# Separate softmax sums for the plain heads, and the last score tile through the fused maximum, in an attention and mixture-of-experts kernel

## The chip, the cores and the metric

The kernel runs on one core of a Trainium2 chip, as one program. The metric is the device time of one execution in microseconds, the median over runs. Names of engines in the profile: PE is TensorE (PEld its weight loads), DVE is VectorE, ACT is ScalarE, POOL is GpSimd, SP is SyncE, which issues most transfers.

## The reference

```python
scores = q @ k^T / sqrt(64)                 # 4 batches, 8 heads, 576 tokens, 64 per head
scores = where(block_i >= block_j, scores, -1e9)   # blocks of 64 tokens
attn = exp(scores - max); attn = attn / (sum + 1e-9); x = attn @ v
x = x as 2304 tokens of 512
h = max(x @ w1, x @ w2, x @ w3); x = h @ w_out     # 512 -> 768 -> 512
logits = x @ w_gate + log1p(exp(x @ w_noise)) * noise
the two highest of 8 experts per token, softmax over the two
out = sum over both of weight * (relu(x @ w1[e]) @ w2[e])   # 512 -> 1024 -> 512
```

All data are fp32. The weights w1, w2, w3 and w_out arrive as 64-bit words, which the kernel turns into fp32 itself.

## The kernel before, in words

The program is written with a framework that places the waits and fixes, when the kernel is built, the order of the instructions on each engine: a planner with its own instruction times takes what is ready, by its place in the program text. The order in the trace is therefore near the text's, but not the same. On the chip each engine runs its queue in that fixed order.

**Attention.** A head has 576 queries. The first 256 (two tiles of 128, the "first" tiles) are computed apart from the rest; tiles 2, 3 and 4 are the head's three score steps. `s1` scores tile 2 against 384 keys, `s3` tile 3 against 512, `s2` tile 4 against 576, in two halves of 288 in a pair of PSUM banks called "a2" (one buffer). `s1` and `s3` share two banks called "s". The block mask is added by a small matmul (line 213) for the plain heads, and by the mask tile in the fused maximum for the others. The mask tile has 512 columns, all zero but for the upper half of the last 64.

Heads 0 to 7 (NF = 8, the first batch) are **plain**: fp32 products, then in `exps` a maximum on VectorE (line 240), a scaling by 0.125 of that maximum (line 241) and an exponential with its sum on ScalarE, read from PSUM (line 242). Heads 8 to 31 are **fused**: products in two fp32r parts, and for `s1` and `s3` one VectorE instruction (line 235) that adds the mask, writes the negated scaled scores to SBUF and keeps their minimum; the exponential then reads SBUF. `s2` takes the maximum and scaling in all heads before.

The three steps of one head share one statistics tile `st` (three buffers), made in `s2`. After the last step, `s3`, `inverse` (lines 245 and 246) adds 1e-9 to three sums and takes three reciprocals, and `scale_by` scales the three tiles: on VectorE (line 253), or on ScalarE (line 251) for `s3` of heads 0 to 2.

**First tiles.** Batch 0 does them for two heads at a time before the loop: `first_scores` (lines 432 to 447) gives four parts to `soft`, four times; `first_rest` turns them, multiplies with the values and writes the input of the gated layer's unit 0. The calls 1 and 3 have the bank pair "a2". Beside heads 1 to 4 `first_scores` runs four times more for batch 1. Batches 2 and 3 use `f_scores` with the fused maximum on two parts.

**The loop over heads** follows ORDER: in iteration i the score steps of head i + 1 and the transposes (`t1`, `t2`) and value products of head i are issued, with gaps ("g") in which weight conversion (`weights`) and, once the first weights are there, the gated layer (`filler`, with units in the order CH, lines 662 to 664) go in. This layer's matmuls are TensorE's filler during attention. Conversion of one piece of weight is a transfer and lines 575 to 588 on VectorE, ScalarE and GpSimd. After the loop come the rest of the gated layer, the routing and the experts (lines 1041 to 1090).

Of the kernel before, what the change touches and what calls it, by code (L numbers as in the profile page):

```python
# [13 lines left out]
AF = mybir.ActivationFunctionType  # L14
OP = mybir.AluOpType
AX = mybir.AxisListType
# [20 lines left out]
NF = 8  # L37
# [4 lines left out]
NRM = (0, 3, 0, 0)  # L42
# [7 lines left out]
NP, NK, NQ = 2, 2, 2  # L50
# [5 lines left out]
def plain(ap):  # L56
    return ap.bitcast(F32)
# [3 lines left out]
def tile_attention_moe_moe(ctx, tc, qT, kT, v, w1, w2, w3, w_out, gates, noise, e1, e2, out):  # L61
    nc = tc.nc
# [28 lines left out]
    mask = consts.tile([128, 512], BF, name="mask")  # L91
# [51 lines left out]
    PA = [att.tile([128, 384], F32, name=f"Pa{j}") for j in range(NP)]  # L143
    PB = [att.tile([128, 1088], F32, name=f"Pb{j}") for j in range(NP)]
# [44 lines left out]
    def prep_head(i):  # L189
        if i < NF:  # L190
            QK[i] = RAW.pop(i)
            return
        q, k = RAW.pop(i)
        Qs = att.tile([128, 384], F32R, name="Qs", bufs=NQ)
        Kh = att.tile([128, S], F32R, name="Kh", bufs=NK)
        Kl = att.tile([128, S], F32R, name="Kl", bufs=NK)
        nc.scalar.activation(Qs, q, AF.Copy)
        nc.scalar.activation(Kh, k, AF.Copy)
        nc.gpsimd.tensor_sub(Qs[64:], q[64:], plain(Qs[64:]))
        nc.gpsimd.tensor_sub(Kl, k, plain(Kh))  # L200
        QK[i] = (Qs, Kh, Kl)
# [9 lines left out]
    def masked(ps, o):  # L211

        nc.tensor.matmul(ps[:, o:o + 64], mL, mask[:, 448:], start=False, stop=True)

    def scores(ps, i, t, k0, k1, diag=None):
        if i < NF:
            q, k = QK[i]
            nc.tensor.matmul(ps, q[:D, 128 * t - 256:128 * t - 128], k[:D, k0:k1], start=True, stop=diag is None)
            if diag is not None:
                masked(ps, diag)  # L220
            return
        Qs, Kh, Kl = QK[i]
        lt = Qs[:, 128 * t - 256:128 * t - 128]
        nc.tensor.matmul(ps, lt, Kh[:, k0:k1], start=True, stop=False)
        nc.tensor.matmul(ps, lt, Kl[:, k0:k1], start=False, stop=True)

    def stats():
        return att.tile([128, 4, 4], F32, name="st", bufs=3)

    def exps(st, j, src, dst, fused):  # L230
        scale = 0.125
        if fused:

            w = src.shape[-1]
            nc.vector.tensor_tensor_reduce(out=dst, in0=src, in1=mask[:, 512 - w:], scale=-scale, scalar=3.0e38,
                                           op0=OP.add, op1=OP.min, accum_out=st[:, 1, j:j + 1])
            src, scale = dst, -1.0
        else:
            ax = AX.XY if len(src.shape) == 3 else AX.X
            nc.vector.tensor_reduce(st[:, 0, j:j + 1], src, axis=ax, op=OP.max, negate=True)  # L240
            nc.vector.tensor_scalar(st[:, 1, j:j + 1], st[:, 0, j:j + 1], scale, None, op0=OP.mult)  # L241
        nc.scalar.activation(dst, src, AF.Exp, bias=st[:, 1, j:j + 1], scale=scale, accum_out=st[:, 2, j:j + 1])

    def inverse(st, n):
        nc.vector.tensor_scalar(st[:, 2, :n], st[:, 2, :n], 1.0e-9, None, op0=OP.add)
        nc.vector.reciprocal(st[:, 3, :n], st[:, 2, :n])
        return st[:, 3]

    def scale_by(st, j, dst, norm=False):
        if norm:  # L250
            nc.scalar.activation(dst, dst, AF.Copy, scale=st[:, 3, j:j + 1])
        else:
            nc.vector.tensor_scalar(dst, dst, st[:, 3, j:j + 1], None, op0=OP.mult)

    def soft(parts, scaled=True, fused=False):
        st = stats()
        for j, (src, dst) in enumerate(parts):
            exps(st, j, src, dst, fused)
        inv = inverse(st, len(parts))
        if not scaled:  # L260

            return inv
        for j, (src, dst) in enumerate(parts):
            scale_by(st, j, dst)

    def bank(kind="m"):
        n, c = TAGS[kind]
        return (psS if n == "s" else psT).tile([128, 512], F32, name=n, bufs=c)


    ST = {}

    def s1(i):
        ps = bank("s")[:, :384]
        scores(ps, i, 2, 0, 384, 320)
        exps(ST[i], 1, ps, PA[i % NP], i >= NF)

    def s3(i):
        Pa, Pb, st = PA[i % NP], PB[i % NP], ST.pop(i)
        ps = bank("s")  # L280
        scores(ps, i, 3, 0, 512, 448)
        exps(st, 2, ps, Pb[:, 576:], i >= NF)

        inverse(st, 3)
        scale_by(st, 0, Pb[:, :576])
        scale_by(st, 1, Pa)
        scale_by(st, 2, Pb[:, 576:], i < NRM[1])

    def s2(i):
        Pb = PB[i % NP]  # L290
        ST[i] = stats()
        ps = psS.tile([128, 2, 512], F32, name="a2")
        scores(ps[:, 0, 0:288], i, 4, 0, 288)
        scores(ps[:, 1, 0:288], i, 4, 288, 576)
        exps(ST[i], 0, ps[:, :, 0:288], Pb[:, :576].rearrange("p (a b) -> p a b", a=2), False)

    POFF = {2: (PA, 0), 3: (PB, 576), 4: (PB, 0)}

# [133 lines left out]
    def first_scores(data, P, two=False, scaled=True):  # L432
        q, k = data[:2]
        parts = []
        if two:
            pair = psS.tile([128, 2, 512], F32, name="a2")
        for r in range(2):
            m = slice(64 * r, 64 * r + 64)
            ps = pair[:, r] if two else bank("s")
            for t in range(2):  # L440
                o = 128 * t
                n = o + 128
                a, b = (q, k[:, r]) if len(k.shape) == 3 else (q[m], k[m])
                nc.tensor.matmul(ps[:, o:o + n], a[:, o:o + 128], b[:, :n], start=True, stop=False)
                masked(ps, o + n - 64)
                parts.append((ps[:, o:o + n], P[:, 384 * r + o:384 * r + o + n]))
        return soft(parts, scaled)


    FR, FQ, FT = {}, {}, []  # L450
# [33 lines left out]
    def f_scores(b, h):  # L484
        Qs, Kh, Kl, _ = FQ[b, h]
        ps = bank("s")
        for t in range(2):
            p, lt = ps[:, 256 * t:256 * t + 256], Qs[:, 128 * t:128 * t + 128]
            nc.tensor.matmul(p, lt, Kh, start=True, stop=False)
            nc.tensor.matmul(p, lt, Kl, start=False, stop=True)  # L490
        soft([(ps[:, 0:128], FP[:, 0:128]), (ps[:, 256:512], FP[:, 128:384])], fused=True)
# [374 lines left out]
    def weights(n):  # L866
        for _ in range(n):
            next(conversion, None)

    weights(1)  # L870
    warm(bank(), WM[0])
    inv = first_scores(FIRST[0], PB[0], A2 & 1, False)
    for j in range(4):
        weights(WS[0])
        if j < 3:
            nxt = first_scores(FIRST[j + 1], PB[(j + 1) % NP], A2 >> (j + 1) & 1, False)
        first_rest(FIRST[j], PB[j % NP], PB[j % NP], 0, j, inv)
        inv = nxt
        weights(WS[1])
# [3 lines left out]
    load_head(1)  # L883
    load_values(1)
    weights(WS[4])
    s2(0)
    s1(0)
    s3(0)
    prep_head(1)
    weights(WS[2])  # L890
    cost = [0.0]
# [21 lines left out]
    for i in range(NH):  # L913
        b, h = divmod(i, H)
# [16 lines left out]
        for o in ORDER.split():  # L931
# [11 lines left out]
            elif o == "pf":  # L943
                if i + 1 in FI:
                    prep_f(*FI[i + 1])
                if i + 2 in FI:
                    load_f(*FI[i + 2])
            elif o == "fs":
                if i in AI:
                    first_scores(later.pop(), FP)  # L950
                    if order:
                        later.append(load_later(*order.pop(0)))
                if i in FI:
                    f_scores(*FI[i])
            elif o == "fr":
                if i - 1 in AI:
                    fb, j = AI[i - 1]
                    first_rest(now.pop(), FP, FP, 2 * fb, j)
                    if j == 3:
                        ready.add(2 * fb)  # L960
                if i in AI:
                    now.append([load_later_v(*AI[i])])
                if i - 1 in FI:
                    f_turn(*FI[i - 1])
            elif o == "fv":
                if i - 1 in FI:
                    f_values(*FI[i - 1])
            elif o[0] == "t":
                (t1, t2)[int(o[1]) - 1](i)
            elif i + 1 < NH:  # L970
                {"s1": s1, "s2": s2, "s3": s3}[o](i + 1)
# [16 lines left out]
    def bank2():  # L988
        turn[0] ^= 1
        if turn[0]:  # L990
            return ps2.tile([128, 512], F32, name="b")
        return psT.tile([128, 512], F32, name="t", bufs=4)
# [150 lines left out]
    ps = bank2()  # L1143
# [77 lines left out]
    with tc.If(full > 0):  # L1221
# [10 lines left out]
        with tc.For_i(0, E) as e:  # L1232
# [4 lines left out]
            with tc.For_i(0, NT) as t:  # L1237
# [6 lines left out]
                ps = ps3.tile([128, 4, 128], F32, name="pa")  # L1244
# [66 lines left out]
```

## Time and profile before

| | |
|---|---|
| median of 3 runs | 1087.37 us (1085.68 to 1087.65) |
| the profiled execution | 1087.95 us, span 1086.1 us |
| mean granted TensorE clock | 0.967 |
| TensorE busy | 1034.8 us (95%) |
| VectorE busy | 537.9 us (50%) |
| ScalarE busy | 459.1 us (42%) |
| GpSimd busy | 533.3 us (49%) |

The span is from the first to the last instruction; the time contains the little around it. Busy shares are means over stages of quite different kind: attention with conversion up to some 216 us, attention with the fused heads up to some 516 us, then the experts.

### The profile page before, as it was taken

What the parts mean: (1) busy time and instruction counts of PE and PEld (TensorE: products, weight loads), DVE (VectorE), ACT (ScalarE), POOL (GpSimd) and SP (SyncE); (2) the same over time, 40 slices, a digit from 0 to 9 for tenths busy, and PEclk for the clock granted to TensorE, in tenths of its full rate; (3) what the DMA queues carried; (4) which work ended last, traced back from release to release, by engine and by line L of the source; (5) the groups of instructions that cost most, each with busy time, mean ns of one, the idle gap of its engine ahead of it and who ended that gap; (6) DMA issues with size and microseconds to landing.
All of it is one profiled execution on the core that took longest, in us unless ns stands there. A gap on an engine that the chain in (4) does not pass through costs nothing. (4 is left out here: it accounts for less than half of the span.)

```text
span 1086.1 us, 18720 instructions
## 1 busy us (share of the span) xinstructions
PE 1034.8 (95%) x6721; PEld 917.4 (84%) x6721; DVE 537.9 (50%) x1552; ACT 459.1 (42%) x1138; POOL 533.3 (49%) x465
## 2 busy tenths in 40 slices
PE   8799999999979999799999999989999999999997
PEld 4466678998879989799999997979898898989895
DVE  7789746596796887756333632222132222222221
ACT  5656555565765666554311433323232322323110
POOL 4447503455556464451321448877474646656302
PEclk7698999998989999899999999999999999999999
DMA  9533312152442323211020236655443444443101
GB/s 232 160 93 125 106 47 63 34 157 58 144 150 65 113 63 100 70 26 39 24 80 21 69 118 206 198 167 169 130 159 121 143 146 146 137 136 114 57 20 63
DMA packets 78513, 115.93 MB, mean 107 GB/s; under 512 B 17976, under 2 KB 48184, under 8 KB 78416
## 3 DMA queue, kind: packets, MB, share of 16 engines
q1 hardware_dynamic: 67824, 85.28, 26.3%
q0 software_dynamic: 10592, 29.41, 8.3%
q8 instruction: 54, 0.88, 0.3%
q14 instruction: 43, 0.35, 0.1%
HBM read 95.18 MB, written 20.53 MB: 107 GB/s over the span
## 5 line engine op out<-in xcount | busy, mean ns | idle before, releaser
L132 POOL TENSOR_TENSOR w<-rw,w 128x1536 fp32r<-128x1536 f32 (+1 forms) x45 | 141.1, 3142 | 74.2 <-ACT w L131 63.9
L131 ACT ACTIVATE w<-rw 128x1536 fp32r<-128x1536 f32 (+1 forms) x45 | 60.2, 1343 | 114.4 <-DMA rw<-in_e 65.0
L662 PE MATMUL t<-xA,w 128*128 128x256 f32 x360 | 105.2, 294 | 1.5 <-ACT w L587 0.8
L664 PE MATMUL t<-xA,w 128*128 128x256 f32 x360 | 103.9, 289 | 0.0
L663 PE MATMUL t<-xA,w 128*128 128x256 f32 x360 | 103.7, 289 | 0.1
L1041 PE MATMUL b<-xh,w 128*128 128x384 f32 (+7 forms) x272 | 86.8, 320 | 0.9 <-ACT xh L1031 0.9
L1042 PE MATMUL b<-xl,w 128*128 128x384 f32 (+7 forms) x272 | 86.9, 320 | 0.2 <-DVE xl L1032 0.2
L1043 PE MATMUL b<-xh,w 128*128 128x384 f32 (+7 forms) x272 | 86.9, 319 | 0.0
L662 PE MATMUL t<-xB,w 128*128 128x256 f32 x288 | 83.7, 291 | 1.4 <-DVE st L241 1.2
L677 POOL TENSOR_TENSOR hl<-hm,hh 128x512 fp32r<-128x512 f32 x24 | 31.6, 1318 | 105.2 <-ACT hh L676 105.2
L663 PE MATMUL t<-xB,w 128*128 128x256 f32 x288 | 82.7, 287 | 0.0
L664 PE MATMUL t<-xB,w 128*128 128x256 f32 x288 | 82.3, 286 | 0.0
L1090 POOL DMA_INDIRECT out_rows<-y,isc x40 | 40.5, 1013 | 79.9 <-DVE y L1089 72.6
L1046 DVE SCALAR_TENSOR_TENSOR ht<-b,ht 128x384 fp32r<-128x384 f32 (+6 forms) x56 | 29.1, 519 | 97.5 <-ACT ht L1045 97.5
L669 DVE TENSOR_TENSOR hm<-t,hm 128x512 f32<-128x512 f32 x54 | 37.2, 690 | 72.1 <-PE t L664 64.1
L662 PEld LDWEIGHTS t<-xA,w 128*128 128x128 f32 x360 | 69.6, 194 | 3.7 <-ACT w L587 0.9
L1085 PE MATMUL b<-w,ht 128*128 128x512 f32 (+1 forms) x168 | 67.1, 400 | 3.6 <-ACT ht L1045 3.6
L664 PEld LDWEIGHTS t<-xA,w 128*128 128x128 f32 x360 | 69.9, 194 | 0.5 <-issue 0.4
L663 PEld LDWEIGHTS t<-xA,w 128*128 128x128 f32 x360 | 69.9, 194 | 0.4 <-POOL xA L516 0.3
L1089 DVE SCALAR_TENSOR_TENSOR y<-b,idt,prev 128x512 f32<-128x512 f32 (+1 forms) x24 | 18.0, 750 | 104.8 <-PE b L1087 83.9
L1043 PE MATMUL t<-xh,w 128*128 128x256 f32 x240 | 67.4, 281 | 0.0
L1042 PE MATMUL t<-xl,w 128*128 128x256 f32 x240 | 67.4, 281 | 0.0
(383 smaller groups left out, 3245.8 us busy)
## 6 DMA issues: line engine op xcount, KB each, us to landing
rw<-in_e SPq DMA_DIRECT2D x32, 768.0 KB
xB<-in_w SPq DMA_DIRECT2D x36, 256.0 KB
rw<-in_e SPq DMA_DIRECT2D x16, 512.0 KB
rk<-in_kT SPq DMA_DIRECT2D x48, 144.0 KB
rq<-in_qT SPq DMA_DIRECT2D x48, 96.0 KB
x2d<-x SPq DMA_DIRECT2D x18, 256.0 KB
out_rows<-x SPq DMA_DIRECT2D x9, 512.0 KB
rv<-in_v SPq DMA_DIRECT2D x24, 160.0 KB
```

Source lines behind the costliest of these rows:

```text
L131: nc.scalar.activation(t[:, 0, :c], r[:, :c], AF.Copy)
L132: nc.gpsimd.tensor_sub(t[:, 1, :c], r[:, :c], plain(t[:, 0, :c]))
L662: nc.tensor.matmul(ps[:, j], wh, x[:, 0], start=kt == 0, stop=False)
L663: nc.tensor.matmul(ps[:, j], wh, x[:, 1], start=False, stop=False)
L664: nc.tensor.matmul(ps[:, j], wl, x[:, 0], start=False, stop=kt == 3)
L669: nc.vector.tensor_max(m, ps, m)
L677: (nc.vector if u == NU - 1 else nc.gpsimd).tensor_sub(l, m, plain(a))
L1041: nc.tensor.matmul(p, wt1(e, 0, kt, f), th[:, kt, c0:c1], start=kt == 0, stop=False)
L1042: nc.tensor.matmul(p, wt1(e, 0, kt, f), tl[:, kt, c0:c1], start=False, stop=False)
L1043: nc.tensor.matmul(p, wt1(e, 1, kt, f), th[:, kt, c0:c1], start=False, stop=kt == 3)
L1085: nc.tensor.matmul(ps, a, wt2(e, 0, f), start=f == 0, stop=False)
L1090: st = nc.gpsimd.indirect_dma_start(out=out, out_offset=bass.IndirectOffsetOnAxis(ap=isc[:n, e, c:c + 1], axis=0), in_=y, in_offset=None, ...
```

## The change

The plain heads' steps each get a statistics tile, a sum and a scaling of their own, through `soft`. In `soft` without fusing, all maxima are taken first, then one scaling over all of them, then all exponentials; this holds for `first_scores` too. The fused heads keep one sum for three tiles, and `s2` uses the fused maximum, with the mask tile's first 288 columns, which are zero, spread over both halves. Before the loop the steps of head 0 stand in the order `s1`, `s3`, `s2`.

```diff
@@ exps
             w = src.shape[-1]
-            nc.vector.tensor_tensor_reduce(out=dst, in0=src, in1=mask[:, 512 - w:], scale=-scale, scalar=3.0e38,
+            m = mask[:, 512 - w:] if len(src.shape) == 2 else mask[:, None, :w].to_broadcast([128, 2, w])
+            nc.vector.tensor_tensor_reduce(out=dst, in0=src, in1=m, scale=-scale, scalar=3.0e38,
                                            op0=OP.add, op1=OP.min, accum_out=st[:, 1, j:j + 1])
@@ soft
-    def soft(parts, scaled=True, fused=False):
-        st = stats()
-        for j, (src, dst) in enumerate(parts):
-            exps(st, j, src, dst, fused)
-        inv = inverse(st, len(parts))
+    def soft(parts, norm=False, scaled=True, fused=False):
+        st, n = stats(), len(parts)
+        if fused:
+            for j, (src, dst) in enumerate(parts):
+                exps(st, j, src, dst, True)
+        else:
+            for j, (src, dst) in enumerate(parts):
+                ax = AX.XY if len(src.shape) == 3 else AX.X
+                nc.vector.tensor_reduce(st[:, 0, j:j + 1], src, axis=ax, op=OP.max, negate=True)
+            nc.vector.tensor_scalar(st[:, 1, :n], st[:, 0, :n], 0.125, None, op0=OP.mult)
+            for j, (src, dst) in enumerate(parts):
+                nc.scalar.activation(dst, src, AF.Exp, bias=st[:, 1, j:j + 1], scale=0.125,
+                                     accum_out=st[:, 2, j:j + 1])
+        inv = inverse(st, n)
...
-            scale_by(st, j, dst)
+            scale_by(st, j, dst, norm)
@@ s1
-        exps(ST[i], 1, ps, PA[i % NP], i >= NF)
+        if i < NF:
+            soft([(ps, PA[i % NP])], i < NRM[0])
+        else:
+            exps(ST[i], 1, ps, PA[i % NP], True)
@@ s3
-        exps(st, 2, ps, Pb[:, 576:], i >= NF)
+        if i < NF:
+            soft([(ps, Pb[:, 576:])], i < NRM[1])
+            return
+        st = ST.pop(i)
+        exps(st, 2, ps, Pb[:, 576:], True)
         inverse(st, 3)
         scale_by(st, 0, Pb[:, :576])
         scale_by(st, 1, Pa)
-        scale_by(st, 2, Pb[:, 576:], i < NRM[1])
+        scale_by(st, 2, Pb[:, 576:])
@@ s2
-        ST[i] = stats()
...
-        exps(ST[i], 0, ps[:, :, 0:288], Pb[:, :576].rearrange("p (a b) -> p a b", a=2), False)
+        part = ps[:, :, 0:288], Pb[:, :576].rearrange("p (a b) -> p a b", a=2)
+        if i < NF:
+            soft([part], i < NRM[2])
+        else:
+            ST[i] = stats()
+            exps(ST[i], 0, *part, True)
@@ before the loop
-    s2(0)
     s1(0)
     s3(0)
+    s2(0)
```

NRM is (0, 3, 0, 0), so `s3` of heads 0 to 2 is still scaled on ScalarE.

## Rows read from the trace of the kernel before

**Rows 1.** The page's busy times and shares of the span, with instruction counts.
```profile
PE 1034.8 (95%) x6721; PEld 917.4 (84%) x6721; DVE 537.9 (50%) x1552; ACT 459.1 (42%) x1138; POOL 533.3 (49%) x465
```

**Rows 2.** Table by stage: length, busy PE, PEld, DVE, ACT, POOL, clock, DMA share, GB/s.
```profile
0.00:54.00 54.00, 42.15 (x152) 25.67 (x153) 39.46 (x123) 33.41 (x98) 24.64 (x35) 0.72 0.73 197
54.00:136.00 82.00, 77.48 (x434) 54.56 (x432) 69.71 (x153) 46.10 (x123) 47.15 (x49) 0.94 0.35 107
136.00:217.00 81.00, 80.95 (x545) 65.91 (x545) 43.62 (x156) 41.61 (x126) 22.25 (x22) 1.00 0.17 48
217.00:516.00 299.00, 278.54 (x2125) 267.94 (x2125) 224.88 (x732) 184.02 (x516) 148.60 (x165) 0.96 0.30 90
516.00:1086.00 570.00, 555.69 (x3473) 503.31 (x3471) 160.20 (x393) 153.92 (x277) 290.69 (x196) 0.99 0.37 115
```

**Rows 3.** TensorE's waits up to 560 us: total us, times, longest.
```profile
PE s L224 <- DVE st L235: 7.5, 4, 4.3
...
PE a L218 <- ACT Pb L242: 2.5, 1, 2.5
```

**Rows 4.** Groups by line and shape up to 520 us: busy us, mean ns, idle before.
```profile
L240 DVE TENSOR_REDUCE st<-a 128x1 f32<-128x576 f32 x32 | 24.0, 750 | 3.9 <-PE a L218 2.6 <-PE a L225 1.0
...
L242 ACT ACTIVATE Pb<-Pb,st 128x512 f32<-128x512 f32 x24 | 17.3, 719 | 2.7 <-DVE st L235 2.7
...
L235 DVE CUSTOM_DVE_ANT_0 Pb<-s,mask 128x512 f32<-128x512 f32 x24 | 16.2, 677 | 0.0
...
L235 DVE CUSTOM_DVE_ANT_0 Pa<-s,mask 128x384 f32<-128x384 f32 x24 | 13.0, 543 | 0.0
...
L241 DVE TENSOR_SCALAR st<-st 128x1 f32<-128x1 f32 x80 | 11.2, 145 | 0.7
...
L245 DVE TENSOR_SCALAR st<-st 128x3 f32<-128x3 f32 x32 | 7.3, 228 | 14.5 <-ACT Pb L242 14.4
...
L235 DVE DVE_READ_ACCUMULATOR2_ANT st<- 128x1 f32 x80 | 6.5, 81 | 0.0
...
L242 ACT ACTIVATE Pb<-s,st 128x512 f32<-128x512 f32 x8 | 5.5, 692 | 3.8 <-DVE st L241 3.5 <-DVE xA L553 0.4
L246 DVE RECIPROCAL st<-st 128x3 f32<-128x3 f32 x32 | 5.5, 173 | 0.7
```

**Rows 5.** Timeline of the start, fourth pair: start us, duration us, instruction.
```profile
30.05 0.28 DVE L240 TENSOR_REDUCE st<-a 128x1 f32<-128x128 f32 x1
...
42.66 0.35 ACT L242 ACTIVATE Pb<-a,st 128x128 f32<-128x128 f32 x1
...
44.91 0.41 DVE L240 TENSOR_REDUCE st<-a 128x1 f32<-128x256 f32 x1
...
45.54 0.47 ACT L242 ACTIVATE Pb<-a,st 128x256 f32<-128x256 f32 x1
...
48.02 0.16 DVE L245 TENSOR_SCALAR st<-st 128x4 f32<-128x4 f32 x1
...
59.69 0.42 DVE L553 TENSOR_TENSOR xA<-Pb,xA 128x256 fp32r<-128x256 f32 x1 [0.78 <-ACT xA L552]
...
60.60 0.39 PE L662 MATMUL t<-xA,w 128*128 128x256 f32 x1
```

**Rows 6.** VectorE's waits up to 225 us: total us, times, longest.
```profile
DVE st L245 <- ACT Pb L242: 6.2, 7, 2.6
...
DVE st L240 <- ACT fP L242: 2.8, 4, 1.0
```

**Rows 7.** ScalarE's waits up to 225 us: total us, times, longest.
```profile
ACT fP L242 <- DVE st L241: 6.4, 2, 3.6
```

**Rows 8.** Table by stage for two low-clock stretches among the fused heads, columns as Rows 2.
```profile
297.00:309.00 12.00, 8.14 (x36) 6.94 (x35) 10.88 (x33) 8.73 (x27) 6.55 (x10) 0.72 0.55 166
...
432.00:450.00 18.00, 11.64 (x60) 9.93 (x61) 17.46 (x64) 10.58 (x29) 7.92 (x9) 0.81 0.33 95
```

More of the change, by code (lines that the diff above doesn't have):

```diff
@@ L275, in s1 @@
         scores(ps, i, 2, 0, 384, 320)
-        exps(ST[i], 1, ps, PA[i % NP], i >= NF)
+        if i < NF:
+            soft([(ps, PA[i % NP])], i < NRM[0])
+        else:
+            exps(ST[i], 1, ps, PA[i % NP], True)
     def s3(i):
-        Pa, Pb, st = PA[i % NP], PB[i % NP], ST.pop(i)
+        Pa, Pb = PA[i % NP], PB[i % NP]
         ps = bank("s")
         scores(ps, i, 3, 0, 512, 448)
-        exps(st, 2, ps, Pb[:, 576:], i >= NF)
+        if i < NF:
[3 more added lines that the diff above has]
+        exps(st, 2, ps, Pb[:, 576:], True)
         inverse(st, 3)
@@ L446, in first_scores @@
                 parts.append((ps[:, o:o + n], P[:, 384 * r + o:384 * r + o + n]))
-        return soft(parts, scaled)
+        return soft(parts, False, scaled)
     FR, FQ, FT = {}, {}, []
```

## The prediction

> **What bounds the kernel now.** I read four views in this order: the page's busy times, the table by stage, what TensorE waited for, and the instruction groups by shape. TensorE is busy 1034.8 of 1086.1 us [rows 1], so the end is set by its own work, by its idle time and by the stretches at half clock; the reader should look for where the last two are. The table by stage [rows 2] puts them: up to 54 us TensorE idles 11.9 us (54 less 42.15) at a mean granted clock of 0.72; from 54 to 136 us 4.5 us at 0.94; from 136 to 217 us nothing (80.95 of 81 at 1.00); from 217 to 516 us 20.5 us at 0.96; after that the edit touches nothing. The first three stages hold the first-batch ("plain") heads and the weight conversion, the fourth the fused heads. VectorE is the engine beside it: 39.5 of 54, 69.7 of 82, 43.6 of 81 and 224.9 of 299 us. TensorE's named waits [rows 3] are few: score tiles whose bank VectorE's fused maximum frees late (7.5 us in 4), and once the bank pair "a2", freed by an exponential (2.5 us). So an edit counts where it makes VectorE deliver earlier or later while TensorE has no matrix work of its own. Against the profiled execution's 1087.95 us the median of the runs shown is 0.58 us lower; I work in the former and subtract that at the end.
>
> **Four-part sums: maxima first, one scaling.** The pair steps of the first tiles call the sum helper with four parts, four times before 54 us and four times beside heads 1 to 4. Before, each part goes maximum, scaling, exponential before the next part's maximum is issued; after, four maxima, one scaling, four exponentials. Removed: three scalings of 145 ns [rows 4], per call 0.44 us, for four calls 1.7 us. Removed too is a round trip. Before, VectorE's second maximum in a bank stands behind ScalarE's exponential of the first part: the exponential that starts at 42.66 us lasts 0.35, and the next maximum comes at 44.91, 1.9 us later [rows 5]; in the quieter stretch later VectorE sat idle 2.8 us in four such waits [rows 6]. Added: behind the last maximum stand four exponentials instead of one, so three more of about 0.6 us (0.35 to 0.47 plus 0.2 to read the sum), 1.8 us. In the start these are covered: the last exponential ended near 46.0 us, and VectorE reached the sum only at 48.02, being busy with conversions [rows 5]. If that cover goes, they cost 1.8 us. What hangs on it is the fourth pair: its result is written at 59.69 us and the first gated layer's products resume at 60.60 [rows 5], the earliest time at which TensorE has filler for all that follows.
>
> **Plain heads: three sums for one.** Per head two more adds (228 ns) and two more reciprocals (173 ns) [rows 4]: 0.80 us on VectorE, 6.4 us over eight heads. And two more places per head where VectorE's add waits for an exponential with everything behind it on VectorE waiting too: weight conversion, the maxima of the gated layer, later score maxima. Before, such waits cost 6.2 us in 7 up to 225 us, 0.89 each, the longest 2.6 [rows 6]. Sixteen more would be 14.2 us if all were as bare. From 136 us on they are hidden by TensorE's own work (idle 0.05 us in 81 [rows 2]); by an estimate from even spacing between 48 and 217 us about half, eight, fall before.
>
> Stage by stage that gives, first, the start: three scalings in four calls -1.7, four small instructions of head 0 +0.8, the round trip ahead of the last sum -1.9, the exponentials 0 behind VectorE's queue: -2.8 us. Bounds: -11.9 (all TensorE's idle time there) and +1.8 (the exponentials uncovered); I take -2.8, nearest to the round trip that the rows show. From 54 to 136 us VectorE gets +3.2 (four heads of 0.80), -1.7 (scalings), -2.8 (round trips) and eight waits, +7.1: +5.8 us. It has 12.3 us free there (82 less 69.71), twice that, so I take 0, between 0 and +5.8; below nothing it would go by the 4.5 us that TensorE idles.
>
> **The order of the first head's steps.** The last tile's step moves behind the other two. It issues no transfer; it moves four score products, a maximum, a scaling and an exponential past the two other steps on TensorE, VectorE and ScalarE, and past nothing on SyncE's or GpSimd's queues. Its bank pair is held by the fourth pair's exponentials anyway [rows 3]. 0 us, at best -2.5 (that wait), at worst +0.9, one more wait of the mean just named. More statistics tiles are alive, with three buffers as before; I have no row for a wait on them and keep it in that +0.9.
>
> **Fused heads: the last tile by the fused maximum.** Per head VectorE loses a 576-column maximum (750 ns) and a scaling (145), and gains a fused maximum with 576 columns and its accumulator read (81). The fused rows, 543 ns at 384 and 677 at 512, give 1.05 ns a column, so 744 at 576 [rows 4]. Net -70 ns, 24 times: -1.7 us. ScalarE's exponential now reads SBUF: at 512 columns 719 ns against 692 from PSUM [rows 4], +27 ns or 0.65 us in all, on an engine busy 184 of 299 us: 0 on the path. The bank pair comes free when VectorE ends and not ScalarE; TensorE never waited for that in this stage [rows 3], so 0. Most of the stage is TensorE-bound; the gain counts where TensorE starves, and there VectorE is the full engine: 10.88 of 12 us from 297 on and 17.46 of 18 from 432 on, with TensorE at 0.72 and 0.81 of its clock [rows 8]. About four heads lie in such stretches (some 50 of 299 us, an estimate from the named two and their like), so -0.3 us. Bounds: one such stretch gone or come: from 297 on 3.9 us idle plus 0.28 of 12 us at half clock, together 7.2 us, either way.
>
> The rows say that reading from SBUF costs ScalarE 27 ns more. [...]
>
> **Sum:** -2.8 + 0 + 0 - 0.3 = -3.1, so 1084.85 against the profiled 1087.95, and 1084.3 against the median.
>
> **Rivals.** *The new sum waits decide.* Place: the conversion stretch, 54 to 136 us. VectorE's queue stops eight more times, conversions come later, and TensorE's first products wait for weights. For it: ScalarE already sat idle 6.4 us in two waits for a scaling that VectorE had queued [rows 7], so queues there do couple; and TensorE's clock there is already 0.94. Against: 12.3 us free. Price +5.8, and the start's gain then goes as well, since the same queue holds it: 1087.95 + 5.8 - 0.3 - 0.58 = 1092.9. It decides as soon as less than half of the waits find other VectorE work.
>
> *Nothing moves.* The start's sums come earlier, but TensorE at half clock is busy with score products anyway and resumes the gated layer no sooner; what VectorE saves and gets in the middle cancels. For it: from 48 to 60 us TensorE is rarely idle. 1087.
>
> *A starved stretch more or less.* The order on each engine is fixed when the kernel is built, by a planner's own times; other instructions give another order, in the fused stage too. A stretch like that from 297 us costs 7.2: 1094.6 with one more on top of nothing gained, 1077.1 with one fewer on top of the forecast. The trace has no second order to compare, so both stay open, the former a little likelier, since each saving is small.
>
> *The edit does not do what it says:* if the planner still interleaves maxima and exponentials, only the scalings go; that is the case "nothing moves".
>
> **Chances.** Forecast 0.38 (its own range 1081 to 1087; 0.05 of it lies within 0.2%), nothing moves 0.18, sum waits 0.24, a stretch more 0.11, a stretch fewer 0.09. A difference under 0.2%, 2.2 us, can't be told from none here. Faster 0.33 + 0.09 = 0.42; same 0.05 + 0.18 = 0.23; slower 0.24 + 0.11 = 0.35. The range must reach both outer cases: 1077 to 1096.
>
> **What would show it.** Right: the four maxima of a pair step stand together on VectorE; the fourth pair's sum comes before 46 us and the gated layer's products resume before 58.5; fused maxima of 576 columns near 744 ns; the stage from 54 to 136 us keeps its idle time within 2 us. Wrong: the idle time before the adds rises by more than 6 us before 136 us with TensorE's clock below 0.9 there (the first rival); TensorE's resumption still near 60.6 us (the second); a low-clock stretch between 217 and 516 us that has no counterpart, or one that is gone (the third).

## The result: 1073.7 us for 1087.5, faster by more than the forecast

The changed kernel takes 1073.74 us in the median of four runs (1071.09 to 1075.49), the kernel before 1087.51 beside it (1085.68 to 1088.87): ratio 0.987, 95% interval 0.985 to 0.989. Measured a second time it took 1076.08 us beside 1086.83, ratio 0.9905 (0.988 to 0.993). So the gain is 11 to 14 us. The forecast was 1084.3 us with 1077 to 1096 around it: the direction and the place were right, the size was not. The profiled execution took 1071.09 us, of which 1069.3 are the span.

The page's busy times after, the line that answers to [rows 1]:
```profile
PE 1020.7 (95%) x6721; PEld 906.3 (85%) x6721; DVE 528.5 (49%) x1560; ACT 457.4 (43%) x1138; POOL 533.2 (50%) x465
```
TensorE executes 6721 instructions as before, yet it is busy 14.1 us less, at a mean granted clock of 0.981 in place of 0.967: a busy time also shrinks when products run at full clock (the two score products at the end of this section: 0.80 us at a granted clock of 0.50, 0.49 at 1.00). Where they do is in the table by stage of the changed kernel, with the columns and limits of [rows 2] (the last stage ends with this span):
```profile
0.00:54.00 54.00, 42.80 (x201) 25.50 (x202) 41.94 (x134) 36.44 (x109) 26.41 (x35) 0.94 0.72 202
54.00:136.00 82.00, 77.07 (x439) 54.84 (x439) 62.10 (x165) 47.48 (x134) 46.91 (x50) 0.94 0.37 109
136.00:217.00 81.00, 80.79 (x569) 68.94 (x568) 48.35 (x171) 43.18 (x128) 27.24 (x28) 1.00 0.22 64
217.00:516.00 299.00, 280.96 (x2180) 270.06 (x2179) 220.96 (x710) 180.59 (x503) 148.25 (x163) 0.97 0.29 85
```
Up to 54 us TensorE idles 11.2 us, against 11.9 before, so hardly less; but it got through 201 instructions in place of 152, at a granted clock of 0.94 in place of 0.72. From 54 to 136 us nothing is different (idle 4.9 against 4.5, clock 0.94 in both). Among the fused heads the idle time is 18.0 us against 20.5.

The gain can be dated by landmarks. The first value product of a fused head, by the line of each kernel in the view of one line (count; shortest, median and longest ns; first and last start in us), before and after:
```profile
L378 PE MATMUL t<-PT,V x240: 191/307/468, 215.6 to 539.6; 128*128 128x320 f32 x72, 128*128 128x256 f32 x24, 128*128 128x64 f32 x24
```
```profile
L400 PE MATMUL t<-PT,V x240: 191/307/472, 205.1 to 523.3; 128*128 128x320 f32 x72, 128*128 128x256 f32 x24, 128*128 128x64 f32 x24
```
At 215 us the changed kernel leads by 10.5 us, at the last of these products by 16.3. All but the last 6 us are won before the first fused head, and from the first expert product to the end both take the same (469.4 before, 469.0 after).

How the first 10 us are won shows in the timeline of the start. The second pair's scores lie in bank pair "a2". Before (start us, duration us, instruction):
```profile
12.28 0.28 DVE L240 TENSOR_REDUCE st<-a 128x1 f32<-128x128 f32 x1
...
13.55 0.35 ACT L242 ACTIVATE Pb<-a,st 128x128 f32<-128x128 f32 x1
...
15.57 0.39 DVE L240 TENSOR_REDUCE st<-a 128x1 f32<-128x256 f32 x1
...
18.28 0.47 ACT L242 ACTIVATE Pb<-a,st 128x256 f32<-128x256 f32 x1
...
19.43 0.28 DVE L240 TENSOR_REDUCE st<-a 128x1 f32<-128x128 f32 x1
...
20.75 0.36 ACT L242 ACTIVATE Pb<-a,st 128x128 f32<-128x128 f32 x1
...
22.03 0.41 DVE L240 TENSOR_REDUCE st<-a 128x1 f32<-128x256 f32 x1
...
23.04 0.48 ACT L242 ACTIVATE Pb<-a,st 128x256 f32<-128x256 f32 x1
...
23.66 0.80 PE L444 MATMUL a<-w 128*128 128x128 f32 x2
```
Maximum, exponential, maximum, exponential: four parts take from 12.28 to 23.61 us (the last exponential with the read of its sum), each handing over between two engines that have other work queued, and only then do the fourth pair's scores get the banks (23.66). After:
```profile
12.70 1.14 DVE L265 TENSOR_REDUCE st<-a 128x1 f32<-128x128 f32 x4
...
15.08 0.16 DVE L266 TENSOR_SCALAR st<-st 128x4 f32<-128x4 f32 x1
...
15.33 0.37 ACT L268 ACTIVATE Pb<-a,st 128x128 f32<-128x128 f32 x1
...
16.48 0.48 ACT L268 ACTIVATE Pb<-a,st 128x256 f32<-128x256 f32 x1
...
17.10 0.49 PE L466 MATMUL a<-w 128*128 128x128 f32 x2 [0.20 <-ACT Pb L268]
...
23.96 1.14 DVE L265 TENSOR_REDUCE st<-a 128x1 f32<-128x128 f32 x4
...
33.41 0.47 ACT L268 ACTIVATE Pb<-a,st 128x256 f32<-128x256 f32 x1
...
36.40 0.16 DVE L247 TENSOR_SCALAR st<-st 128x4 f32<-128x4 f32 x1
...
50.42 0.41 DVE L575 TENSOR_TENSOR xA<-Pb,xA 128x256 fp32r<-128x256 f32 x1
51.22 0.28 PE L684 MATMUL t<-xA,w 128*128 128x256 f32 x1
```
The same four parts take from 12.70 to 17.05: the work passes between the two engines once, not seven times. The banks are free 6.6 us earlier, and the fourth pair's first maximum stands at 23.96 in place of 30.05. The fourth pair's own parts are shorter by as much again: from that maximum to the end of the last exponential 9.9 us (33.88, the row at 33.41) in place of 16.0 (46.01 [rows 5]). So its sum stands at 36.40 in place of 48.02, the last input of the gated layer's first unit at 50.42 in place of 59.69 [rows 5], and behind it the filler products resume, at 51.22 in place of 60.60; a few had run ahead of it in both kernels. The two score products of one row show the clock as well: 0.80 us at 23.66 before (granted clock 0.50 from 23 to 26 us), 0.49 at 17.10 after (1.00 from 17 to 19 us).

### The profile page after: what moved, and what is told of

It is laid out like the page before. It is cut to its first block, busy times and chain, and to the rows that moved or that the text cites. A ratio compares the mean times of both kernels' runs of the same rounds, so it can differ in the third digit from the quotient of the medians.

```text
span 1069.3 us, 18712 instructions
## 1 busy us (share of the span) xinstructions
PE 1020.7 (95%) x6721; PEld 906.3 (85%) x6721; DVE 528.5 (49%) x1560; ACT 457.4 (43%) x1138; POOL 533.2 (50%) x465
## 5 line engine op out<-in xcount | busy, mean ns | idle before, releaser
L684 PE MATMUL t<-xA,w 128*128 128x256 f32 x360 | 104.4, 292 | 0.1
L685 PE MATMUL t<-xA,w 128*128 128x256 f32 x360 | 102.4, 285 | 0.7 <-DVE xA L575 0.4
L686 PE MATMUL t<-xA,w 128*128 128x256 f32 x360 | 102.5, 285 | 0.0
L691 DVE TENSOR_TENSOR hm<-t,hm 128x512 f32<-128x512 f32 x54 | 37.3, 690 | 72.9 <-PE t L686 62.8
L684 PEld LDWEIGHTS t<-xA,w 128*128 128x128 f32 x360 | 68.6, 191 | 1.9 <-issue 0.8
L685 PEld LDWEIGHTS t<-xA,w 128*128 128x128 f32 x360 | 68.7, 191 | 1.5 <-DVE xA L575 0.5
L686 PEld LDWEIGHTS t<-xA,w 128*128 128x128 f32 x360 | 68.5, 190 | 0.4 <-POOL w L610 0.3
```

Of the source, the lines that this page charges most:

```text
L684: nc.tensor.matmul(ps[:, j], wh, x[:, 0], start=kt == 0, stop=False)
L685: nc.tensor.matmul(ps[:, j], wh, x[:, 1], start=False, stop=False)
L686: nc.tensor.matmul(ps[:, j], wl, x[:, 0], start=False, stop=kt == 3)
L691: nc.vector.tensor_max(m, ps, m)
```

## The experiments

A "landmark" below is the start of the first value product of a fused head in the run's profile (215.6 us before, 205.1 after). The "fourth pair's sum" is the add behind its four exponentials, the "last input" the write of its result [rows 5]; both, the landmark and any clock are read from the one profiled execution of each kernel, while the times are medians. Ratios are to the kernel before, run beside it, with 95% intervals. In "maxima first" the four-part helper computes all maxima, then one scaling, then all exponentials, as in the change.

**Maxima first in the four calls of the start alone** (kernel before otherwise):
```diff
-        for j, (src, dst) in enumerate(parts):
-            exps(st, j, src, dst, fused)
+        if fused or not first: ...
+        else:
+            (maxima; one scaling; exponentials)
...
-        return soft(parts, scaled)
+        return soft(parts, scaled, first=not scaled)
```


> The kernel before, with maxima first and one scaling only in the four pair calls ahead of the loop (batch 0); all else as before. Theory A (the start's round trips between VectorE and ScalarE made the whole gain of the start): fourth pair's input written near 49 us instead of 59.7, mean granted clock up to 54 us near 0.94 instead of 0.72, total 9 to 12 us under before, near 1077. Rival B (the plain heads' own sums and the new order of head 0's steps free the start): under 3 us gained, fourth pair still after 57 us. Rival C (any other order shifts by some us either way): the start as in B, the total anywhere within 8 us.

Measured 1077.85 us against 1086.77, ratio 0.992 (0.989 to 0.994), landmark 207.8, the fourth pair's sum at 36.2 us, the last input at 51.7, the granted clock up to 54 us 0.89. These four calls alone give about 9 us (6 to 12 by the interval).

**Maxima first in the other four calls alone**, beside heads 1 to 4: as above with `first=scaled`.

> The kernel before, with maxima first only in the four pair calls beside heads 1 to 4. A: the start unchanged up to 60 us; total within 2 us of before, since TensorE was full from 136 us on. B: the same. C: anywhere within 8 us of before although the start is unchanged, by another order among the fused heads.

1086.14 us, ratio 0.9996 (0.998 to 1.001), landmark 215.7. The same edit, four times, is worth nothing to within 2 us where TensorE has filler.

**Three sums and the new order of head 0 alone** (the changed `s1`, `s2`, `s3`, with the old helper and the old maximum):
```diff
-        exps(ST[i], 1, ps, PA[i % NP], i >= NF)
+        if i < NF:
+            soft([(ps, PA[i % NP])])
+        else:
+            exps(ST[i], 1, ps, PA[i % NP], True)
...
-    s2(0)
     s1(0)
     s3(0)
+    s2(0)
```


> The kernel before, with separate sums for the plain heads and head 0's steps in the order tile 2, 3, 4; pair calls interleaved as before, last tile of the fused heads not fused. A: the start changes by less than 2 us, total within 3 us of before (more likely slower by the added waits). B: fourth pair's input written by 52 us, total 9 us or more under before. C: the start little changed, the total within 8 us either way.

1088.42 us, ratio 1.000 (0.998 to 1.002), landmark 215.0. Within 2.4 us they neither cost nor give anything, so the first rival (the new sum waits decide, priced at 5.8 us) falls.

**The fused last tile alone**:
```diff
-            nc.vector.tensor_tensor_reduce(out=dst, in0=src, in1=mask[:, 512 - w:], ...
+            m = mask[:, 512 - w:] if len(src.shape) == 2 else mask[:, None, :w].to_broadcast([128, 2, w])
+            nc.vector.tensor_tensor_reduce(out=dst, in0=src, in1=m, ...
...
-        exps(ST[i], 0, ps[:, :, 0:288], ..., False)
+        exps(ST[i], 0, ps[:, :, 0:288], ..., i >= NF)
```


> The kernel before, with the last tile of the fused heads by the fused maximum only. Up to 180 us nothing should differ by more than 1 us. If the 6 us that the changed kernel gained between 217 and 450 us come from the fused maximum itself, the total is 4 to 7 us under before; if they come from an order that fits by luck (C), it is anywhere from 5 under to 7 over; if from VectorE's 70 ns per head alone, 0 to 2 under.

1083.91 us, ratio 0.997 (0.995 to 0.999), landmark 216.5: about 3 us, all behind the landmark.

**The changed kernel with the four parts interleaved again**:
```diff
-            (maxima; one scaling; exponentials)
+            for j, (src, dst) in enumerate(parts):
+                exps(st, j, src, dst, False)
```


> The changed kernel with its pair calls interleaved as before (maximum, scaling, exponential, part by part); sums apart and the fused last tile kept. Theory A (start by maxima first, about -9 us; fused last tile about -3): total 1082 to 1085, fourth pair's input written near 60 us. Rival B (the parts work together, sums apart are needed for the gain): under 1079 or over 1087.

1085.62 us against 1088.31, ratio 0.997 (0.995 to 0.999), landmark 218.5, fourth sum at 47.2 us, last input at 59.9. What is left of the change is the fused tile's 3 us.

**The changed kernel without the fused last tile**:
```diff
-            exps(ST[i], 0, *part, True)
+            exps(ST[i], 0, *part, False)
```


> The changed kernel with the fused heads' last tile by maximum, scaling and exponential from PSUM as before. A: 3 us above the changed kernel, 1076 to 1078, the start as in the changed kernel. Rival (an order that fits by luck): any sign, and the low-clock stretches among the fused heads at other places.

1079.22 us, ratio 0.990 (0.987 to 0.994), landmark 210.4. The interval overlaps that of the change, so the fused tile's part is not told apart here. Nor does the late landmark tell: up to 173 us the four engines run the changed kernel's instructions in the changed kernel's order, so what is late there from the start (last input at 55.5, granted clock 0.75 up to 54 us) is this execution and not the edit.

**Maxima first in all eight calls and the fused tile, but joint sums and the old order.**

> The kernel before with all pair calls maxima first and the fused last tile; one sum for three tiles of the plain heads and the old order of head 0's steps kept. A: equal to the changed kernel within 2 us, 1072 to 1076, since sums apart are worth nothing by themselves. Rival B: 4 us or more above the changed kernel.

1080.87 us, ratio 0.993 (0.989 to 0.997), landmark 209.3. The expectation, 1072 to 1076 us, was missed: the median is some 5 us slower than the parts, added, would give. The interval contains that of the maxima alone, lies just above the changed kernel's first one (0.985 to 0.989) and overlaps its second (0.988 to 0.993). So it stays open whether separate sums, worth nothing by themselves, are worth something beside the other parts.

**Maxima first in the start, with four scalings kept**: the first experiment's kernel with
```diff
-            nc.vector.tensor_scalar(st[:, 1, :len(parts)], st[:, 0, :len(parts)], 0.125, None, op0=OP.mult)
+            for j in range(len(parts)):
+                nc.vector.tensor_scalar(st[:, 1, j:j + 1], st[:, 0, j:j + 1], 0.125, None, op0=OP.mult)
```


> The kernel of the first experiment (maxima first in the four pair calls ahead of the loop) but with four scalings of one column instead of one of four columns, still between the maxima and the exponentials. Theory A1 (the round trips): within 1.5 us of that experiment, 1077 to 1080. Rival A2 (VectorE's twelve fewer instructions): back at 1083 to 1087.

1076.98 us, ratio 0.989 (0.985 to 0.992), landmark 205.6. Nothing is seen to be lost with the scalings back; the intervals, 3 to 4 us either way, are too wide to exclude the 1.7 us that the forecast gave the twelve that go.

**Two maxima, a scaling and two exponentials for each bank**, in the start alone:
```diff
+            for h in (0, 2):
+                for j in (h, h + 1): (maximum)
+                (one scaling of two columns)
+                for j in (h, h + 1): (exponential)
```


> The kernel before; in the four pair calls ahead of the loop two maxima, one scaling and two exponentials for one bank, then the same for the other, so no maximum waits behind an exponential of its own bank, but the second bank's maxima are issued after the first bank's exponentials. If the round trip inside a bank is what the start lost, this gives most of it: fourth pair's sum by 41 us, its input by 54 us, total within 3 us of the first experiment's 1077.9. If all four maxima have to stand together, the fourth input stays after 56 us and the total is 1082 or more.

1077.46 us against 1086.83, ratio 0.993 (0.990 to 0.996), landmark 206.8. Its timeline for the second pair:
```profile
12.46 0.61 DVE L263 TENSOR_REDUCE st<-a 128x1 f32<-128x128 f32 x2
...
13.94 0.37 ACT L266 ACTIVATE Pb<-a,st 128x128 f32<-128x128 f32 x1 [0.18 <-DVE st L264]
...
17.55 0.61 DVE L263 TENSOR_REDUCE st<-a 128x1 f32<-128x128 f32 x2
...
18.88 0.37 ACT L266 ACTIVATE Pb<-a,st 128x128 f32<-128x128 f32 x1 [0.95 <-DVE st L264]
...
19.85 0.49 PE L453 MATMUL a<-w 128*128 128x128 f32 x2 [2.02 <-ACT Pb L266]
```
Two parts of a bank stand together, and the second bank follows the first as before: three handovers in place of seven. The banks come free at 19.85, between 17.10 and 23.66, the fourth pair's sum stands at 37.3 and the last input at 51.6, and the gain is that of the first experiment. So it is enough to take the exponential from between the two maxima of one bank; that all four maxima stand together is not needed.

**The kernel before with sixteen idle products in the start**, to keep TensorE busy while the pairs run:
```diff
-WM = (14, 0, 0, 0, 0)
+WM = (14, 0, 2, 0, 0)
```


> The kernel before with two dense 512-column bf16 matmuls on ones, which no one reads, ahead of the transposes of each half pair in the start (16 in all), so that TensorE is kept busier there; nothing else changed. If the half clock was the cause of the start's loss and the VectorE chain only went along (rival K): granted clock up to 54 us 0.85 or more and the fourth pair's input 5 us or more earlier, total 1079 to 1082. Theory A (the chain over VectorE and ScalarE sets the start and TensorE's clock follows its gaps): fourth input still at 58 to 61 us whatever the clock, total within 4 us of before.

1094.35 us, ratio 1.007 (1.006 to 1.009), landmark 222.1. The table by stage for its start:
```profile
0.00:54.00 54.00, 42.64 (x167) 24.99 (x168) 38.54 (x123) 33.24 (x98) 24.93 (x35) 0.81 0.70 197
```
The granted clock rises from 0.72 to 0.81, and the last input still stands at 60.7 us. The run gives no support to the rival that the low clock makes the start late, but it is a weak test: the clock did not reach the 0.85 at which the rival was to be judged, and the added products, some 8 us of TensorE (13.0 us against 4.9 of such products up to 54 us), sit in the same chain, so a part of the price is theirs. The other runs say more. Up to 54 us, in the other four calls alone and in the changed kernel without the fused tile:
```profile
0.00:54.00 54.00, 37.51 (x155) 23.08 (x156) 41.85 (x124) 33.47 (x98) 25.03 (x35) 0.84 0.69 197
```
```profile
0.00:54.00 54.00, 45.84 (x170) 26.21 (x171) 40.19 (x119) 33.18 (x100) 24.64 (x35) 0.75 0.69 193
```
The first has the parts interleaved and the higher clock, 0.84, and its landmark is 215.7; the second has maxima first and 0.75, and its landmark is 210.4.

**The changed kernel with the pair calls by the fused maximum**, mask added by VectorE in place of the mask products:
```diff
-                nc.tensor.matmul(ps[:, o:o + n], a[:, o:o + 128], b[:, :n], start=True, stop=False)
-                masked(ps, o + n - 64)
+                nc.tensor.matmul(ps[:, o:o + n], a[:, o:o + 128], b[:, :n], start=True, stop=True)
...
-        return soft(parts, False, scaled)
+        return soft(parts, False, scaled, True)
```


> The changed kernel, and the pair calls too use the fused maximum with the mask tile (scores written to SBUF, no mask matmul, no scaling; exponentials read SBUF), in all eight calls. It takes 32 mask matmuls from TensorE and the scalings from VectorE, and frees the score banks when VectorE ends. Theory A: the fourth pair's sum comes no later than in the changed kernel (36.4 us), total 1 to 4 us under the changed kernel. Rival: writing the scores makes each VectorE step wait for the buffer that the pair before still uses, so the start is longer: fourth input after 53 us, total 2 to 6 us over the changed kernel.

1080.19 us, ratio 0.994 (0.992 to 0.996): as medians 4 us slower than the changed kernel beside it, whose interval (0.988 to 0.993) it just touches. Landmark 210.4, the fourth pair's sum at 37.0, the last input at 52.7, and the clock from 54 to 136 us is 0.88. Why it is slower is not shown.

**The changed kernel again**, beside the three above:

> The changed kernel itself, on the same chip as the three beside it, to compare with them: 12 to 15 us under before, as measured already, 0.985 to 0.989 of it.

1076.08 us, ratio 0.9905 (0.988 to 0.993), landmark 207.6.

That settles the start, and not the fused tile: forecast -0.3 us, measured near -3 alone. Three more kernels take its possible causes one by one, and a fourth undoes the order of head 0.

**Four extra scalings of VectorE behind each fused last tile**, and **one**:
```diff
-            exps(ST[i], 0, *part, True)
+            exps(ST[i], 0, *part, True); [nc.vector.tensor_scalar(ST[i][:, 0, 0:1], ST[i][:, 1, 0:1], 0.125, None,
+                                          op0=OP.mult) for _ in range(4)]
```


> The changed kernel with four more one-column scalings of 145 ns on VectorE behind each fused last tile: 0.58 us a head, 13.9 us in 24 heads, eight times what the fused maximum saved there. Theory A (the fused tile's 3 us is VectorE's time in starved stretches): the rate would be 3 us for 1.7, so 14 us or more are lost, 1088 or above. Theory B (only starved stretches count, about a sixth of the stage): 2 to 3 us, 1076 to 1079. Theory C (it is the bank pair that comes free at VectorE's end, or only another order): within 2 us of the changed kernel, 1072 to 1077.

> The same with one such scaling a head, which puts back the time of the removed one: 3.5 us in 24 heads. Theory A: 3.5 to 6 us lost, 1077.5 to 1081. Theory B: under 1 us. Theory C: under 1 us by the work, but if the order that the edit brings decides, up to 3 us either way, and not between the changed kernel and the one with four.

With four: 1074.4 us against 1087.7, ratio 0.987 (0.985 to 0.990), landmark 207.0. With one: 1073.79 us, 0.9875 (0.986 to 0.989), landmark 207.0. The added work in the first, by form up to 517 us, and its stage of the fused heads:
```profile
L317 DVE TENSOR_SCALAR st<-st 128x1 f32<-128x1 f32 x96 | 13.9, 144 | 0.9
```
```profile
217.00:516.00 299.00, 279.57 (x2153) 268.07 (x2152) 224.65 (x799) 182.28 (x510) 148.15 (x165) 0.97 0.29 86
```
13.9 us more on VectorE, the time is not worse, and TensorE is busy 279.57 us of the stage in place of 280.96. So 13.9 us of VectorE's time, put there, cost at most some 3 us; the 1.7 us that the fused tile saves on VectorE can't by themselves be worth 3.

**The bank pair held until ScalarE has read it**, by a read of one column behind the exponential:
```diff
-            exps(ST[i], 0, *part, True)
+            exps(ST[i], 0, *part, True); nc.scalar.activation(ST[i][:, 0, 0:1], ps[:, 0, 0:1], AF.Copy, scale=1.0)
```


> The changed kernel with a read of one column of the last tile's bank pair by ScalarE behind its exponential, so that the pair comes free at ScalarE's end, as before the change; it costs some 0.2 us of ScalarE a head. If the early release is what gains: 3 us lost, 1077 to 1078. If it is VectorE's time: within 1 us of the changed kernel, 1073 to 1076. If it is the order: up to 3 us either way.

1075.35 us, ratio 0.989 (0.987 to 0.991), landmark 206.5: inside what the changed kernel itself shows (0.987 and 0.9905). Beside the two kernels above, run with it, it is 1 to 1.6 us slower, within the intervals: the early release is worth that or nothing.

**The changed kernel with head 0's steps in the old order**:
```diff
+    s2(0)
     s1(0)
     s3(0)
-    s2(0)
```


> The changed kernel with the first head's steps in the old order, last tile first. Theory: nothing, 1073 to 1077, since the step moves past nothing but its own head's two other steps. Rival: the new order takes the wait for the bank pair away and is worth up to 2.5 us: 1076 to 1079.

1075.65 us, ratio 0.989 (0.987 to 0.991): the same. Its landmark is late for its group, 211.5, and so is the execution that was profiled, 1080.5 us, the slowest of the six. One profile's landmark is good to a few microseconds.

The landmarks of all kernels that keep the pairs' work as before or as changed, with the time from there to the first expert product:
```
maxima first in the start         landmark us   to the experts us
  changed, again                  205.1, 207.6    395.2, 396.5
  start alone                     207.8           398.1
  start alone, four scalings      205.6           398.9
  start alone, per bank           206.8           397.1
  all eight + fused               209.3           401.0
  changed, not fused              210.4           400.3
  changed + 4, + 1 scalings       207.0, 207.0    398.4, 397.2
  changed, late release           206.5           397.4
  changed, old order              211.5           397.8
interleaved in the start
  before                          215.6           401.1
  other four calls                215.7           397.9
  sums apart                      215.0           398.0
  fused alone                     216.5           395.3
  changed, interleaved            218.5           398.5
```
The first column falls into two groups that don't meet: a mean of 207.7 us (205.1 to 211.5, 11 profiles) and of 216.3 (215.0 to 218.5, 5), 8.6 us apart. The second column does not: with the fused tile it is 397.5 in the mean (395.2 to 401.0, 9), without it 398.8 (397.1 to 401.1, 7). The kernel before happens to have the longest of all and the changed one the shortest.

How far one execution moves the first column is seen in six of these profiles: of the changed kernel (twice), without the fused tile, with four and one more scalings, and with the late release. On TensorE, VectorE, ScalarE and GpSimd they run the same instructions in the same order up to 173 us. Their landmarks go from 205.1 to 210.4, their last inputs from 50.4 to 55.5, and their granted clocks up to 54 us from 0.75 to 0.94, the one at 0.75 being the latest. So of the 10.5 us between the two profiles of the result, some 5 can be the execution, and the 8.6 us between the means is the better figure.

## Why the prediction was wrong

**The start, -2.8: this step failed.** Its bounds were -11.9 and +1.8, and it took -2.8 as "nearest to the round trip that the rows show". The rows that it read were those of the last call [rows 5], and it counted the round trip once, ahead of the last sum. But each of the four calls has it, and the calls are chained by the bank pair: while the second pair's parts alternate between the engines, the fourth pair has no banks. The timelines price it: 11.3 us for the second pair's four parts before and 4.4 after, 16.0 and 9.9 us for the fourth pair's own. Measured for the four calls: 8.6 us at the landmark, and about 9 in the time of the kernel with nothing else changed. Two other terms of the start are not seen in the runs, which can't tell terms that small from nothing: the scalings, -1.7 (four scalings kept: 0.989), and head 0's small instructions, +0.8 (sums apart: 1.000). That the later exponentials are covered was right: the sum came earlier, not later.

There was a sign of it in the views. [rows 3] names TensorE's wait for that bank pair, "PE a L218 <- ACT Pb L242", 2.5 us, and the prediction used it for the order of head 0 instead of asking why an exponential holds that bank so late. And the far bound read the 11.9 us idle up to 54 us as the most that could be gained; the idle time stayed, 11.2 us, and the gain came as filler that resumes 9 us earlier. The higher clock, 0.94 for 0.72, goes along in this profile, but with four extra scalings it is 0.84 and the landmark is 207.0.

**54 to 136 us, 0: right.** Idle 4.9 against 4.5 us. The waits of the added sums came to less than feared. VectorE's waits up to 225 us after (total us, times, longest), to be read beside [rows 6]:
```profile
DVE st L247 <- ACT Pa L268: 2.2, 4, 0.8
...
DVE st L247 <- ACT Pb L244: 1.8, 3, 1.0
...
DVE st L247 <- ACT Pb L268: 1.1, 2, 0.6
```
5.1 us in 9 where sixteen more were feared, and the maxima's 2.8 us in 4 have no line left.

**The order of head 0's steps, 0: right** to within 2 us (0.989 with the old order).

**The fused heads, -0.3: the direction right, the size open.** The parts were as read. By form, up to 517 us:
```profile
L237 DVE CUSTOM_DVE_ANT_1 Pb<-a,mask 128x576 f32<-128x576 f32 x24 | 17.8, 743 | 0.0
L265 DVE TENSOR_REDUCE st<-a 128x1 f32<-128x576 f32 x8 | 6.0, 745 | 0.3 <-PE a L218 0.3
```
```profile
L244 ACT ACTIVATE Pb<-Pb,st 128x576 f32<-128x576 f32 x24 | 18.6, 773 | 3.5 <-DVE st L237 3.1
L268 ACT ACTIVATE Pb<-a,st 128x576 f32<-128x576 f32 x8 | 6.1, 759 | 0.0
```
743 ns where 744 were worked out, and the exponential that reads SBUF takes 14 ns more than the one that reads PSUM in the same kernel, less than the 27 taken from the 512-column rows. On an engine busy 181 of 299 us neither decides anything. In time the fused tile alone measured 3 us (1.5 to 5.5), and taken out of the change it left 0.990 beside 0.987 and 0.9905. Neither VectorE's time nor the early release is seen to carry that by itself: 13.9 us put on VectorE lost nothing that shows, and the late release 1 to 1.6 us as medians. By the table of landmarks the tile is worth 1.3 us on a spread of 4 to 6. What may be left is another order of the instructions, since an edit gives one: TensorE's products stand in the changed kernel's order up to 255 us in the changed kernel without the fused tile, and not behind that. That the order makes the 3 us is not shown; no run changes the order and nothing else, and the cause stays open. Both low stretches of [rows 8] are still there, 15 us earlier, in the table by stage after:
```profile
282.00:300.00 18.00, 13.29 (x73) 10.85 (x72) 17.72 (x56) 13.26 (x40) 10.68 (x13) 0.81 0.74 235
...
417.00:435.00 18.00, 11.62 (x69) 10.47 (x69) 15.56 (x55) 10.18 (x27) 8.53 (x10) 0.81 0.26 74
```
VectorE is full in the first, as before, and the prediction read it as the limit there. That TensorE waits for VectorE's fused maxima is so. From 217 to 516 us (total us, times, longest), in the changed kernel and with four extra scalings a head:
```profile
PE s L224 <- DVE st L237: 6.5, 3, 3.6
```
```profile
PE s L224 <- DVE st L237: 6.6, 4, 3.2
```
But 13.9 us more of small work did not lengthen that wait, so 70 ns saved a head, counted at full value in such stretches, is not what the runs support.

**The rivals.** "The sum waits decide" (0.24) fell with the sums alone, "nothing moves" (0.18) with the start alone. "A stretch fewer" lies nearest in time (1077.1), but no stretch is gone: the start made the gain. The measured 1073.7 lies under the range because the outer case was built on -2.8. With the start's own bound, -11.9, that case would have come to 1068.0 and held it; the bound alone, with no stretch fewer, gives 1075.2, and the rest is the fused tile.

## What to carry to other kernels

Where several parts share a bank and go through two engines, count the handovers of the whole chain, and ask who waits for the bank at its end; put the maxima of a bank together before its first exponential. Here the same edit was worth 9 us where TensorE had no filler yet and nothing, to within 2 us, where it had. A term with wide bounds belongs into the range with its far end.

## What the runs showed of the hardware

- A maximum of one part of a bank waited for the exponential of another part of the same bank, though both only read: 2.8 us in four such waits [rows 6], and none left when the maxima go first. What orders them is not the statistics tile, which both write. The first call of the kernel before has its parts in two banks "s" and one statistics tile:
```profile
7.62 0.29 DVE L240 TENSOR_REDUCE st<-s 128x1 f32<-128x128 f32 x1
7.64 0.37 ACT L242 ACTIVATE Pb<-s,st 128x128 f32<-128x128 f32 x1 [5.61 <-PE s L213]
...
7.91 0.19 ACT L242 ACTIVATION_READ_ACCUMULATOR Pb<-s,st 128x1 f32 x1
...
8.13 0.42 DVE L240 TENSOR_REDUCE st<-s 128x1 f32<-128x256 f32 x1
```
  The maximum at 7.62 is the other bank's and runs beside the first bank's exponential; the first bank's second maximum starts at 8.13, when that exponential and the read of its sum have ended (8.10). That leaves the bank. Whether the chip or the program's own ordering asks for it was not tried.
- Back to back on one bank pair VectorE's four maxima take 1.14 us (0.28 and 0.41 apiece before), one group of records.
- 96 more instructions of 144 ns on VectorE in a stage where it is three quarters busy (224.65 of 299 us) cost nothing that shows, 1074.4 us against 1073.79 with a quarter as many.
- TensorE's granted clock in the start is not steady from execution to execution: 0.75 to 0.94 up to 54 us in six profiles with the same instructions in the same order up to 173 us, and 0.72 and 0.84 in the kernel before and with maxima first in the other four calls, the same up to 77 us, with the landmark at 215.6 and 215.7. So a clock of one profiled start is worth little by itself.
